# 1 KB weight rows with four open tiles, the gate sums on their own, half of the LayerNorm on ScalarE, and QK half by half

## The chip, the cores and the metric

The kernel runs on one core of one Trainium2 chip. The metric is the device time of one execution in microseconds (us). The kernel before takes 165.44 us, the median of 12 runs that lie between 165.05 and 165.8.

A core has five engines that each follow their own instruction list in order: TensorE (PE, with its weight loads shown apart as PEld), VectorE (DVE), ScalarE (ACT), GpSimd (POOL) and SyncE (SP). They wait for each other by semaphores. SP, ACT and POOL also issue DMAs.

## The reference

The input `x` has 2048 tokens of 512 features in bf16. Two branches are mixed by a gate per token:

```python
g = _sigmoid((x * gate_w).sum(-1, keepdims=True))
a = _A_ref(x, A_wqkv, A_wo)     # local attention
b = _B_ref(x, B_w1, B_b1, B_w2, B_b2)   # MLP over the tokens
return g * a + (1 - g) * b
```

Branch A projects `x` to Q, K and V (32 heads of 16 features). Each token attends to 8 positions: itself and the tokens 2, 4, ... 14 before it. The 8 logits go through a softmax, and the weighted sum of V is multiplied with `wo`. Branch B takes the LayerNorm of `x` over its features, and then mixes tokens: `u = gelu(h^T w1 + b1)` with `w1` of 2048 x 1792, and `y = u w2 + b2` with `w2` of 1792 x 2048.

## The kernel before, in words

The whole problem lies in SBUF at once. The program adds every operation with its engine, its reads and writes and a guessed duration to a scheduler (`_Sched`), which orders the operations on each engine by its guesses, with priorities (`prio`). What comes out is one fixed list per engine, and waits where an operand comes from elsewhere. TensorE's own operations are chained in the order in which they were added (`PE`), apart from the gate and logit sums (`f_sum`), which the scheduler places.

**TensorE** does, in order: a warm-up, transposes of the first tokens, the Q, K and V projections (L649, 176 matmuls of 128x128x512, four to a PSUM bank, each bank followed by a copy out on ACT), the first MLP matmul (L858, operations `ph2_ft_half`: 14 column tiles `ft`, each of two halves of 8 matmuls over the 2048 tokens), the second one (L885, `ph3_i_half`: 16 token tiles, each of two halves of 7 matmuls) and, into the same PSUM bank, the product with `wo` (L894, `wo0` to `wo15`, 4 matmuls each). ACT takes a finished bank out: `gel0` to `gel13` apply the GELU after `ph2`, and `ev0` to `ev15` finish an output tile, which SP stores.

**VectorE** does the attention by itself. Partitions are 32 heads times 4 of a head's 16 features, and `dl` counts the other 4, so that Q K products are elementwise: `qk h_dl_s` multiplies Q with the 8 shifted K for token half h, feature index dl and half s of those 1024 tokens, in 128x4096 elements (512 tokens times 8 shifts). Buffers are P0, P1, P2, each of two halves. The four `dl` are summed by `qa` adds, of which the first two of token half 0 are done by an accumulating DMA on POOL (L747, `qd0_0` and `qd0_1`) instead. `sum0` and `sum1` on TensorE (L722) then add over the 4 partitions of a head, into PSUM banks 4 to 7; 16 matmuls of 32x512 each. The gate's matmuls (L717, 16 of them, bank 3) go in the same operation as `sum0`. ACT copies the logits out (`lev0`), DVE masks them, takes the maximum and subtracts it (`msk`, `mx4`, `mx2`, `mx1`, `msub`), ACT takes the exponential (`exp0`), DVE sums the 8 (`sm4`, `sm2`, `sm1`), ACT takes the logarithm (`lns0`), DVE adds the gate's part (`rsz0`), ACT takes the exponential (`rb0`) and DVE scales (`nrm0`). The same follows for token half 1. `nrm` releases four DMAs on POOL (L790, `av`) that spread the weights, and then DVE multiplies with V (`avm0` to `avm7`, 128x8192) and adds (`ava`, `avb`, `avc`); for u = 3, 4, 5 POOL does the first addition by DMA (L827, `avd`). `wo` of tiles 2u and 2u+1 needs `avc` of u.

DVE also takes the LayerNorm statistics (L692) and applies it to the 16 token tiles (L706, `ln0` to `ln15`).

**ACT's tables**: GELU needs another table set than logarithm and exponential; a load (L954) stands before each change of set. Copy, Relu and Identity need none of their own.

**Weights**: W1 comes in 7 tiles of 256 columns, all 2048 rows (`w1_0` to `w1_6`), and W2 in 8 tiles of 256 columns (`w2_0` to `w2_7`), all on SP's queue in order. `w1_1` and `w1_2` wait for `qd0_1`; `w1_3` and `w1_4` go into the room of the transposed input XT, which the gate's matmuls and the last V projection must have left; `w1_5`, `w1_6` and the W2 tiles go where earlier tiles were. `ebt` is a DMA transpose of the gate's exponentials, also on SP.

PSUM has 8 banks. Q, K and V copies go round over 7 banks, and over banks 0, 1, 2 in the last twelve V projections. `ph2` goes round over 1, 2, 0 (and 3), one open tile after the other:

```python
MLPB = [1, 2, 0, 1, 2, 0, 3, 1, 2, 0, 3, 1, 2, 0]
for ft in range(NFT):
    bank = MLPB[ft]
    for half in range(2):
        PE(f_ph2(ft, bank, half), 1.735, ...)
```

Of the kernel before, what the change touches and what calls it, by code (L numbers as in the profile page):

```python
# [69 lines left out]
class _Sched:  # L70
# [73 lines left out]
    def _pass(self, ops, extra, dma_bw, dma_lat):  # L144
# [21 lines left out]
        dma_free = 0.0  # L166
# [8 lines left out]
        while nleft:  # L175
            best = None
            for e in self.ENGS:
                lst = ready[e]
                if not lst:
                    continue  # L180
                bo = None
                bk = None
                for op in lst:
                    st = max(clock[e], rtime[op.idx])
                    if op.table is not None and loaded is not None and op.table != loaded:
                        st += 1.3
                    k = (st, -bl[op.idx] + 3.0 * op.prio, op.idx)
                    if bk is None or k < bk:
                        bk = k
                        bo = op  # L190
                if best is None or bk < best[0]:
                    best = (bk, bo)
            assert best is not None, "scheduler deadlock (cyclic deps?)"
            st = best[0][0]
            op = best[1]
            e = op.eng
            ready[e].remove(op)
            op.start = st
            if op.table is not None:
                loaded = op.table  # L200
            if op.is_dma:
                clock[e] = st + op.dur
                xs = max(st + 0.3, dma_free)
                xd = max(op.nbytes / dma_bw, 0.05)
                dma_free = xs + xd
                op.end = max(dma_free, clock[e]) + dma_lat
            else:
                op.end = st + op.dur
                clock[e] = op.end
            order[e].append(op)  # L210
            nleft -= 1
            for s_ in op.succ:
                s_.npend -= 1
                if s_.npend == 0:
                    rt = 0.0
                    for d in s_.deps:
                        lat = 0.06 if (d.eng != s_.eng or d.is_dma) else 0.0
                        rt = max(rt, d.end + lat + s_.delay)
                    for d in s_.order:
                        rt = max(rt, d.start + 1e-4)  # L220
                    rtime[s_.idx] = rt
                    ready[s_.eng].append(s_)
# [85 lines left out]
def bass_gated_mix__sliding_local_dilated__mixer_token_mlp__prompt_kernel(nc, A_x, A_wqkv, A_wo, B_x, B_w1, B_b1, B_w2, B_b2, gate_w, out, dbg=None):  # L308
    with contextlib.ExitStack() as es:
# [11 lines left out]
        for b in range(3):  # L321
# [42 lines left out]
        W1H = [view(n_, BF16, [(256, NST), (1, 256)], extra=k_ * W1N)  # L364
               for n_, k_ in (("W1", 0), ("W1", 1), ("W1", 2), ("XT", 0), ("XT", 1), ("W1", 0), ("W1", 1))]
        W1R = ["w1s0", "w1s1", "w1s2", "w1x0", "w1x1", "w1s0", "w1s1"]

        def w2view(name, extra=0):
            return view(name, BF16, [(256, NFT), (1, 256)], extra=extra)
# [166 lines left out]
        def ld_w1(j):  # L536
            w1ld[j] = load("w1_%d" % j, W1H[j], w1v[:, :, 256 * j:256 * j + 256], S * 256 * 2, [W1R[j]] + (XTALL if j in (3, 4) else []), order=j < 3,
                           after=[w1ld[j - 1]] if j > 3 else [])

        def ld_w2(j):  # L540
            w1ld[7 + j] = load("w2_%d" % j, W2S[j], w2v[:, :, 256 * j:256 * j + 256], F * 256 * 2, ["w2_%d" % j] + W2ALIAS[j], order=False,
                               after=[w1ld[6 + j]])
# [162 lines left out]
        for t in range(NST):  # L705
            A("dve", (lambda t_: lambda e: e.tensor_scalar(out=X[:, t_, :], in0=X[:, t_, :], scalar1=col(RSTD, t_), scalar2=col(NMR, t_),  # L706
                                                           op0=ALU.mult, op1=ALU.add))(t), 0.33,
              reads=["rstd", "nmr", "st%d" % t], writes=["x%d" % t], name="ln%d" % t, prio=-10)


        def f_sum(h, b0, with_gate):
            def fn(e):
                ins = None
                if with_gate:
                    for dt in range(4):
                        for c in range(4):
                            ins = e.matmul(ps[32 * c:32 * c + 32, 3, :], lhsT=GWREP[:, dt, :],  # L717
                                           rhs=sub(XT, dt * S + c * UT_, [(HS, 2), (1, UT_)]),
                                           start=(dt == 0), stop=(dt == 3), tile_position=(0, 32 * c))
                for wp in range(4):  # L720
                    for c in range(4):
                        ins = e.matmul(ps[32 * c:32 * c + 32, 4 + wp, :], lhsT=RP, rhs=sub(PB[b0], (c // 2) * 4096 + 2 * wp * 512 + (c % 2) * UT_, [(512, 2), (1, UT_)]),  # L722
# [4 lines left out]
        LGB = ["b4", "b5", "b6", "b7"]  # L727
        PLAN = {0: (0, 1, 2), 1: (1, 2, 0)}
        PS = [["p%d_%d" % (b_, s_) for s_ in range(2)] for b_ in range(3)]
        qkd = {}  # L730
        for h in range(2):
            bb = PLAN[h]

            def qk(dl, b_, s_, h=h):
                sb = 2 * h + s_
                A("dve", tt(sub(PB[b_], s_ * 4096, [(512, NW), (1, 512)]), sub(QH[h], dl * HS + s_ * 512, [(0, NW), (1, 512)]),
                            sub(KH[h], dl * KR + PAD + s_ * 512, [(-2, NW), (1, 512)]), ALU.mult), 2.25,
                  reads=["q%d_%d" % (dl, sb), "k%d_%d" % (dl, sb)] + (["k%d_%d" % (dl, sb - 1)] if s_ else ["khalo" if h else "kpad"]),
                  writes=[PS[b_][s_]], name="qk%d_%d_%d" % (h, dl, s_))

            def qadd(x_, y_, s_, h=h):
                A("dve", tt(sub(PB[x_], s_ * 4096, [(1, 4096)]), sub(PB[x_], s_ * 4096, [(1, 4096)]), sub(PB[y_], s_ * 4096, [(1, 4096)]), ALU.add), 2.25,
                  reads=[PS[y_][s_]], writes=[PS[x_][s_]], name="qa%d_%d%d_%d" % (h, x_, y_, s_))
# [12 lines left out]
            for s_ in range(2):  # L756
                qk(3, bb[1], s_)
                qadd(bb[2], bb[1], s_)
            for s_ in range(2):
                qadd(bb[0], bb[2], s_)  # L760
            b0 = bb[0]
            A("pe", f_sum(h, b0, h == 0), 1.2 + (1.0 if h == 0 else 0), reads=PS[b0] + ["rp"] + ((XTALL + ["gwrep"]) if h == 0 else []),
              writes=LGB + (["b3"] if h == 0 else []), name="sum%d" % h, prio=-100, delay=0.2)
            if h == 0:
                A("act", act(E32, ps[:, 3, :], AF.Relu, scale=-1.0, bias=ZMAX), 0.6, reads=["b3"], writes=["e32"], name="zclip")
                A("act", act(EB, E32, AF.Exp, scale=-1.0, bias=ZMAX), 0.6, reads=["e32"], writes=["eb"], name="zexp", table=LOGEXP)
# [16 lines left out]
            A("dve", tt(ATT[h], ATT[h], sub(RB, 0, [(0, NW), (1, UT_)]), ALU.mult), 1.2, reads=["rb"], writes=["att%d" % h], name="nrm%d" % h, prio=-30)  # L783
# [26 lines left out]
        AVB = (2, 0, 1)  # L810
        avlast = [None]

        def AV(fn, dur, **kw):
            avlast[0] = A("dve", fn, dur, after=[avlast[0]] if avlast[0] else [], **kw)

        def av_parts(u):
            b_ = AVB[u % 3]
# [36 lines left out]
        def f_ph2(ft, bank, half):  # L854
            def fn(e):
                ins = None
                for st in range(8 * half, 8 * half + 8):
                    ins = e.matmul(ps[:, bank, :], lhsT=W1H[ft // 2][:, st, 128 * (ft % 2):128 * (ft % 2) + 128], rhs=X[:, st, :],  # L858
                                   start=(st == 0), stop=(st == NST - 1))
# [3 lines left out]
        MLPB = [1, 2, 0, 1, 2, 0, 3, 1, 2, 0, 3, 1, 2, 0]  # L863
        for ft in range(NFT):
            bank = MLPB[ft]
            for half in range(2):
                PE(f_ph2(ft, bank, half), 1.735, ["x%d" % t for t in range(8 * half, 8 * half + 8)] + [W1R[ft // 2]], ["b%d" % bank],
                   "ph2_%d_%d" % (ft, half))
            A("act", act(UT[:, ft, :], ps[:, bank, :], AF.Gelu_apprx_tanh, bias=col(B1C, ft)), 0.7,
              reads=["b%d" % bank, "b1c"], writes=["ut%d" % ft] + (["wq0", "wq1", "wq2", "wq3", "wk0", "wk1", "wv"] if ft == 0 else []), name="gel%d" % ft, table=GELU)  # L870
            if ft % 2 == 1 and ft // 2 + 5 <= 6:
                ld_w1(ft // 2 + 5)
# [4 lines left out]
        LAG = 5  # L877
        ring[0], ring[1] = 0, [3, 4, 5, 6, 7, 1, 2, 0]
        banks = {}

        def f_ph3(i, bank, half, c0=0, c1=D):
            def fn(e):
                ins = None
                for ft in range(7 * half, 7 * half + 7):
                    ins = e.matmul(ps[:, bank, 0:c1 - c0], lhsT=W2S[i // 2][:, ft, 128 * (i % 2):128 * (i % 2) + 128], rhs=UT[:, ft, c0:c1],  # L885
# [16 lines left out]
        def finish_tile(i):  # L902
            bank = banks[i]
# [5 lines left out]

        L = NST - 1  # L910
        for i in range(L):
            banks[i] = bank_()
        head = ((0, 0), (1, 0), (2, 0), (0, 1), (1, 1), (2, 1))
        for i, half in head + tuple((i, half) for i in range(3, L) for half in range(2)):
            bank = banks[i]
            PE(f_ph3(i, bank, half), 1.52, ["ut%d" % ft for ft in range(7 * half, 7 * half + 7)] + ["w2_%d" % (i // 2)], ["b%d" % bank], "ph3_%d_%d" % (i, half))
            if half == 1 and i >= LAG:
                finish_tile(i - LAG)
        lastb = [bank_(), bank_()]
        CH = ((0, 384), (384, 512))  # L920
        for hf, (c0, c1) in enumerate(CH):
            for half in range(2):
                PE(f_ph3(L, lastb[hf], half, c0, c1), 0.77, ["ut%d" % ft for ft in range(7 * half, 7 * half + 7)] + ["w2_%d" % (L // 2)], ["b%d" % lastb[hf]],
                   "ph3_%d_%d" % (L, half))
        for i in range(L - LAG, L):
            finish_tile(i)
# [92 lines left out]
```

## Time and profile before

| what | value |
|---|---|
| median of 12 runs | 165.44 us (165.05 to 165.8) |
| the profiled execution, its own time | 165.73 us |
| its span | 164.0 us |
| TensorE's granted clock | 1.0 throughout |
| PE busy | 159.4 us, 97% of the span |
| DVE busy | 150.6 us, 92% |
| ACT busy | 70.2 us, 43% |
| DMA moved | 32.24 MB, 197 GB/s on the mean |
| packets under 2 KB | 42,244 of 44,684 |

The profile is of one execution. The span runs from the first to the last instruction that the profile has; the execution's own time has 1.7 us more around it. Busy shares are means over stages with different limits, so that what bounds a stage is read from that stage's waits and not from this table.

### The profile page before, as it was taken

How to read it: one execution, taken by the hardware profiler on the slowest of the kernel's cores; microseconds unless marked ns; L12 is line 12 of the kernel's file. 1: busy time of each engine (PE TensorE's matmuls, PEld its weight loads, DVE VectorE, ACT ScalarE, POOL GpSimd, SP SyncE). 2: the span in 40 equal slices, each digit the busy share in tenths (PEclk: the TensorE clock that was granted, in tenths of full speed). 3: DMA queues.
4: the chain of work that ended last, by engine and by line, in shares of the span. 5: the costliest groups of instructions: out<-in, count | busy, mean ns of one | idle time of the engine just before them, and what ended most of it. 6: DMA issues, size and time to landing. Idle time of an engine off the chain costs nothing.

```text
span 164.0 us, 1989 instructions
## 1 busy us (share of the span) xinstructions
PE 159.4 (97%) x793; PEld 77.5 (47%) x808; DVE 150.6 (92%) x126; ACT 70.2 (43%) x100; POOL 12.0 (7%) x36
## 2 busy tenths in 40 slices
PE   7999999999999999999999999999999999999993
PEld 3755555555544444444444344444444444444641
DVE  0489999899999999999999999999999999999960
ACT  3357677766772379853211257111121111111164
POOL 3000030020000000004000000002200222000000
DMA  5999969809499094999998974990998899991014
GB/s 154 276 242 276 238 155 288 169 0 192 92 301 309 8 249 125 227 290 290 317 240 256 271 203 138 294 240 8 289 229 211 195 208 199 208 215 37 32 58 134
DMA packets 44684, 32.24 MB, mean 197 GB/s; under 512 B 7940, under 2 KB 42244, under 8 KB 44676
## 3 DMA queue, kind: packets, MB, share of 16 engines
q1 hardware_dynamic: 41444, 22.06, 51.9%
q0 software_dynamic: 2512, 9.44, 27.3%
q10 hardware_dynamic: 720, 0.62, 1.1%
q8 instruction: 6, 0.10, 0.2%
q14 instruction: 2, 0.02, 0.0%
HBM read 18.88 MB, written 2.10 MB: 128 GB/s over the span
## 4 chain that ended last, share of the span: by engine, by line
PE 85%; DMA 6%; SPq 6%; ACT 1%; issue 1%
PE ps L858 29%; PE ps L885 29%; PE ps L649 17%; PE ps L894 8%; DMA arena<-in_A_x_dram 6%; SPq L493 4%; SPq L494 1%; PE ps L722 1%; ACT arena L453 1%; PE ps L717 1%; PE ps L604 0%
## 5 line engine op out<-in xcount | busy, mean ns | idle before, releaser
L450 DVE TENSOR_TENSOR arena<-arena 128x4096 bf16<-128x4096 bf16 (+8 forms) x79 | 131.9, 1718 | 1.6 <-ACT arena L453 0.6
L885 PE MATMUL ps<-arena 128*128 128x512 bf16 (+2 forms) x234 | 50.0, 366 | 0.2
L858 PE MATMUL ps<-arena 128*128 128x512 bf16 x218 | 48.5, 379 | 0.3
L453 ACT ACTIVATE arena<-ps,arena 128x512 bf16<-128x512 f32 (+1 forms) x30 | 21.9, 732 | 60.7 <-PE ps L894 37.7
L453 ACT ACTIVATE arena<-ps 128x512 bf16<-128x512 f32 (+3 forms) x53 | 32.9, 629 | 18.4 <-PE ps L649 10.8
L649 PE MATMUL ps<-arena 128*128 128x512 bf16 x173 | 38.0, 379 | 0.2
L885 PEld LDWEIGHTS ps<-arena 128*128 128x128 bf16 x238 | 22.8, 98 | 25.9
L858 PEld LDWEIGHTS ps<-arena 128*128 128x128 bf16 x224 | 21.7, 98 | 26.9 <-issue 0.8
L649 PEld LDWEIGHTS ps<-arena 128*128 128x128 bf16 x176 | 19.9, 113 | 18.0
L894 PE MATMUL ps<-arena 128*128 128x512 bf16 (+2 forms) x67 | 15.6, 366 | 0.1
L453 ACT ACTIVATE arena<-arena 128x16 f32<-128x16 f32 (+5 forms) x10 | 6.7, 678 | 9.7 <-DVE arena L450 9.6
L954 ACT ACT_TABLE_LOAD x7 | 9.0, 1283 | 2.8 <-issue 2.7
L894 PEld LDWEIGHTS ps<-arena 128*128 128x128 bf16 x68 | 6.5, 98 | 7.3
L790 POOL DMA_DIRECT2D arena<-arena x8 | 4.3, 559 | 75.1 <-DVE arena L450 75.1
L692 DVE BATCH_NORM_STATS2 arena<-arena 128x6 f32<-128x512 bf16 x16 | 9.8, 679 | 0.0
L706 DVE TENSOR_SCALAR arena<-arena 128x512 bf16<-128x512 bf16 x16 | 5.3, 406 | 0.0
L579 DVE COPY arena<-ps 128x256 bf16<-128x256 bf16 x4 | 1.1, 292 | 4.5 <-PE ps L567 4.4
L827 POOL DMA_DIRECT2D arena<-arena x3 | 3.6, 1209 | 17.7 <-DVE arena L450 17.7
L747 POOL DMA_DIRECT2D arena<-arena x2 | 2.5, 1268 | 31.6 <-DVE arena L692 21.1
L588 PE MATMUL ps<-arena 128*128 128x256 bf16 (+1 forms) x27 | 4.5, 319 | 0.2
L588 PEld LDWEIGHTS ps<-arena 128*128 128x128 bf16 x28 | 3.1, 121 | 1.1 <-DVE arena L579 0.4
L551 PE MATMUL ps<-const-bfloat16-1.0 128*128 128x512 bf16 (+1 forms) x9 | 2.7, 483 | 0.9 <-PEq L1004 0.9
(30 smaller groups left out, 14.4 us busy)
## 6 DMA issues: line engine op xcount, KB each, us to landing
arena<-in_B_w_dram SPq DMA_DIRECT2D x7, 1024.0 KB, 6.8
arena<-in_B_w_dram SPq DMA_DIRECT2D x8, 896.0 KB, 9.9
arena<-arena POOLq DMA_DIRECT2D x5, 1024.0 KB, 9.6
arena<-arena POOLq DMA_DIRECT2D x8, 512.0 KB, 11.7
out_dram<-arena SPq DMA_DIRECT2D x15, 128.0 KB, 3.1
arena<-in_A_x_dram SPq DMA_DIRECT2D x3, 512.0 KB, 4.7
arena<-in_A_wqkv_dram SPq DMA_DIRECT2D x2, 256.0 KB, 4.4
arena<-in_A_wqkv_dram SPq DMA_DIRECT2D x1, 512.0 KB, 6.5
```

The costliest lines, as they stand in the source:

```text
L450: return lambda e: e.tensor_tensor(out=o_, in0=a_, in1=b_, op=op_)
L453: return lambda e: e.activation(out=o_, in_=i_, func=f_, **kw)
L493: return e.dma_start_transpose(dst, src)
L588: ins = e.matmul(ps[:, dl, c0:c1], lhsT=sub(WQKV, dt * 3 * D + dl, [(4, 128)]), rhs=XT[:, dt, c0:c1], start=(dt == 0 and hb == 0), stop=(d ...
L649: ins = e.matmul(ps[:, bank, :], lhsT=sub(WQKV, dt * 3 * D + tn * D + dl, [(4, 128)]), rhs=XT[:, dt, sb * 512:(sb + 1) * 512], start=(dt = ...
L692: A("dve", (lambda t_: lambda e: e.bn_stats(out=ST6[:, t_, :], in_=X[:, t_, :]))(t), 0.67, reads=["x%d" % t], writes=["st%d" % t], name="s ...
L706: A("dve", (lambda t_: lambda e: e.tensor_scalar(out=X[:, t_, :], in0=X[:, t_, :], scalar1=col(RSTD, t_), scalar2=col(NMR, t_), op0=ALU.mu ...
L790: prev = sch.dma("pool", (lambda d_, s_: lambda e: e.dma_start(d_, s_))(dst, src), 524288, sch.dsem("av%d_%d" % (h, c)), issue=1.0, reads= ...
L858: ins = e.matmul(ps[:, bank, :], lhsT=W1H[ft // 2][:, st, 128 * (ft % 2):128 * (ft % 2) + 128], rhs=X[:, st, :], start=(st == 0), stop=(st ...
L885: ins = e.matmul(ps[:, bank, 0:c1 - c0], lhsT=W2S[i // 2][:, ft, 128 * (i % 2):128 * (i % 2) + 128], rhs=UT[:, ft, c0:c1], start=(ft == 0) ...
L894: ins = e.matmul(ps[:, bank, 0:c1 - c0], lhsT=OT[:, i // 2, dl, 128 * (i % 2):128 * (i % 2) + 128], rhs=WO[:, dl, c0:c1], start=False, sto ...
L954: e.preload_act_table_set(want)
```

## The change

- W1 from the second tile on, and W2, are loaded as tiles of 512 columns and half of the contraction (8 of 16 row blocks for W1, 7 of 14 for W2). A tile keeps its bytes and its place; a row of it is 1 KB where it was 512 B.
- The matmuls follow that: after `ph2_0` and `ph2_1`, groups of four column tiles are run with half 0 for all four and then half 1 for all four, so that four PSUM banks are open. `ph3` goes the same way in groups of four token tiles; the last four are written out by hand (`TAILORDER`).
- The gate's matmuls become an operation of their own (`gate`), added before QK, with `zclip` and `zexp` after it. `sum0` is left with its 16 matmuls. The logit buffers are laid out so that a sum reads 512 contiguous elements.
- `ln8` to `ln15` go to ACT with a scale and a bias from SBUF; `ln0` to `ln7` stay on DVE with a higher priority.
- `qk` and `qa` are added half by half and have priorities. `avm3` stands after `nrm1`; AV buffers are given out in another order.
- The scheduler's model is changed: separate free times for POOL's and the other DMAs, and another rule for which ready operation comes first on ACT.

In the order that comes out, TensorE has the gate between the projections `pjk2_2` and `pjk2_3`, and `sum0` after `ph2_0_0`, `ph2_0_1`, `ph2_1_0` (before: after `ph2_0` and `ph2_1` whole); `sum1` comes before `ph2_13_0`. SP has `ebt` ahead of `w1_1` (before: after `w1_4`). DVE has, after `ln_nmr`: `ln0` to `ln7`, `qk0_0_1`, three small copies (L682 to L684), `qk0_3_0` (which waits for `qd0_0`), `qk0_1_1` (which releases `qd0_1`), `qa0_21_0`, `qa0_02_0`, `qk0_2_1`, `qk1_0_0`, `qk0_3_1` (which waits for `qd0_1`), `qa0_21_1`, `qa0_02_1` (which releases `sum0`), `qk1_1_0`, `qa1_12_0`, `msk` to `msub0`, `qk1_2_0`, `qk1_3_0`, `sm4_0` to `sm1_0`. ACT has `gel0`, `lev0`, `gel1`, `exp0`, `lns0`, `gel2`, `gel3`, `rb0`, `gel4`, `gel5` there, with a table load at each change of set. POOL keeps its list.

```diff
-            return view(name, BF16, [(256, NFT), (1, 256)], extra=extra)
+            return view(name, BF16, [(512, NFT // 2), (1, 512)], extra=extra)
...
-            w1ld[j] = load("w1_%d" % j, W1H[j], w1v[:, :, 256 * j:256 * j + 256], S * 256 * 2, [W1R[j]] + (XTALL if j in (3, 4) else []), order=j < 3,
+            src = w1v[:, 8 * ((j - 1) % 2):8 * ((j - 1) % 2) + 8, 256 + 512 * ((j - 1) // 2):768 + 512 * ((j - 1) // 2)] if j else w1v[:, :, 0:256]
+            w1ld[j] = load("w1_%d" % j, W1H[j], src, S * 256 * 2, [W1R[j]] + (XTALL if j in (3, 4) else []), order=j < 3,
...
         for t in range(NST):
+            if t >= NST - 8:
+                A("act", act(X[:, t, :], X[:, t, :], AF.Identity, scale=col(RSTD, t), bias=col(NMR, t)), 0.6,
+                  reads=["rstd", "nmr", "st%d" % t], writes=["x%d" % t], name="ln%d" % t, prio=8)
+                continue
...
+        A("pe", f_gate, 1.0, reads=XTALL + ["gwrep"], writes=["b3"], name="gate", prio=-100)
+        A("act", act(E32, ps[:, 3, :], AF.Relu, scale=-1.0, bias=ZMAX), 0.6, reads=["b3"], writes=["e32"], name="zclip")
+        A("act", act(EB, E32, AF.Exp, scale=-1.0, bias=ZMAX), 0.6, reads=["e32"], writes=["eb"], name="zexp", table=LOGEXP)
...
             for s_ in range(2):
                 qk(2, bb[2], s_)
-            for s_ in range(2):
                 qk(3, bb[1], s_)
                 qadd(bb[2], bb[1], s_)
-            for s_ in range(2):
                 qadd(bb[0], bb[2], s_)
...
-            A("pe", f_sum(h, b0, h == 0), 1.2 + (1.0 if h == 0 else 0), reads=PS[b0] + ["rp"] + ((XTALL + ["gwrep"]) if h == 0 else []),
-              writes=LGB + (["b3"] if h == 0 else []), name="sum%d" % h, prio=-100, delay=0.2)
+            A("pe", f_sum(b0), 1.0, reads=PS[b0] + ["rp"], writes=LGB, name="sum%d" % h, prio=-100, delay=0.2)
...
-        MLPB = [1, 2, 0, 1, 2, 0, 3, 1, 2, 0, 3, 1, 2, 0]
+        def mlp1(ft, half):
+            bank = (0, 1, 2, 3, 0, 1, 2, 3, 0, 1, 2, 3, 0, 1)[ft]
...
+        for ft in range(2):
+            for half in range(2):
+                mlp1(ft, half)
+        ld_w1(5)
+        for g_ in range(3):
+            for half in range(2):
+                for ft in range(2 + 4 * g_, 6 + 4 * g_):
+                    mlp1(ft, half)
...
+        for b_ in range(3):
             for half in range(2):
+                for i in range(4 * b_, 4 * b_ + 4):
+                    mlp2(i, half)
+                    if half and b_:
+                        finish_tile(i - 4)
```

## The prediction

> **What bounds the kernel now.** I read the page's busy times first, then the chain that ended last in order of time, then each engine's timeline.
>
> ```profile
> PE 159.4 (97%) x793; PEld 77.5 (47%) x808; DVE 150.6 (92%) x126; ACT 70.2 (43%) x100; POOL 12.0 (7%) x36
> PE 85%; DMA 6%; SPq 6%; ACT 1%; issue 1%
> ...
> 47.80 4.32 PE ps L858 x20
> 52.12 0.05 issue
> 52.17 2.54 PE ps L858 x11
> 54.71 0.98 PE ps L717 x16
> 55.68 0.86 PE ps L722 x16
> 56.55 1.40 PE ps L858 x6
> ...
> 92.91 0.98 PE ps L722 x16
> ```
>
> The chain (start, length, what) is TensorE from 19.7 us to 160.5 with no gap but 0.05 us after every 50 or so matmuls. 32 matmuls take 54.71 - 47.80 = 6.91 us, 0.216 each; the 84 from 99.18 to 117.31 (one record is missing) take 0.216 too. So TensorE runs at its own pace in every stage, and DVE at 92% is not waited for: its attention ends at 158.4 (the row that starts at 152.28 lasts 6.13), 1.2 us before `wo14` needs it (156.19 plus 16 of L894's matmuls is 159.65). **The change can win only what it takes out of TensorE's list, and it takes out nothing. It can lose wherever an operand comes late.**
>
> **The Trainium skill.** "TensorE: Matmul & The Clock Gate", section "Back-to-back issue gap", gives N/2.4 + 2.5 ns for an isolated warm matmul, 216 ns for N = 512. The trace agrees (0.216); the 131 ns that the section names for a stream is nowhere in it. "ScalarE: Activation LUTs", section "What ACT_TABLE_LOAD costs", has 1283 ns for a table load and 1380 for a drain. The first is in this trace; the second isn't, as the rows below show. "DMA: Bandwidth & Descriptors", section "Issuing engines are not separate DMA queues", says that all DMAs share the same 16 engines; here the accumulating DMA of POOL took 9.6 us beside W1's first tile and 8.0 alone.
>
> ```profile
> L954 ACT ACT_TABLE_LOAD x7 | 9.0, 1283 | 2.8 <-issue 2.7
> ...
> 71.48 0.42 ACT L453 ACTIVATE arena<-arena 128x256 bf16<-128x256 f32 x1 [2.02 <-DVE arena L450]
> 71.92 1.28 ACT L954 ACT_TABLE_LOAD   x1
> 73.21 1.43 ACT L453 ACTIVATE arena<-ps,arena 128x512 bf16<-128x512 f32 x2
> ...
> 23.34 1.32 POOL L747 DMA_DIRECT2D arena<-arena  x1 [21.12 <-DVE arena L692]
> 35.14 1.21 POOL L747 DMA_DIRECT2D arena<-arena  x1 [10.47 <-DVE arena L450]
> ...
> DMA to landing us min/median/max: 8.0/8.8/9.6
> ```
>
> ACT's timeline: `rb0` ends at 71.90 and the GELU starts at 73.21, so a change of set costs 1.31. POOL's: `qd0_1` lands at 35.14 + 8.0 = 43.15, where SP's waiting W1 load starts; so the 9.6 belongs to `qd0_0`, which lands at 32.98.
>
> **The change, part by part.**
>
> *Gate alone.* Gate and `sum0` together take 0.98 + 0.86; `sum1`, standing alone, takes 0.98. Parted, each costs 0.98: **+0.12 us** on the path. No row shows a lower price; ends 0 and 0.2. The gate's new place makes it wait for the copy L684, done at 31.6; TensorE is there at 33.2 (30.59 and 12 matmuls), so that wait is hidden.
>
> *TensorE's clock.* The gate moves all before `ph2` by 0.98: `ph2_0_0` at 48.78. `sum0` comes after 24 matmuls, 48.78 + 5.18 = 53.96, and ends at 54.94.
>
> *DVE up to `sum0`.* Eight L706 steps are gone: 11 take 3.64 us with 0.40 for the last, 0.324 each, so 2.59 is saved. From 26.46, `ln0` to `ln7` end the stage at 29.05. A 4096-element op steps by 2.20 (starts 32.55, 34.75, 36.96), by 2.31 where the next one needs it. `qk0_0_1` 29.05 to 31.25; the copies L682 to L684 0.37, 31.62. Now `qk0_3_0` needs `qd0_0`, landed at 32.98: **1.4 us of the saving is waited away**. It starts at 33.01, `qk0_1_1` at 35.21, ending 37.49. `qd0_1` is issued 0.31 later as before (34.83 to 35.14), 37.80, and lands at 45.8. Meanwhile `qa0_21_0` 37.41, `qa0_02_0` 39.72, `qk0_2_1` 41.93, `qk1_0_0` 44.13; `qk0_3_1` at 46.33 finds `qd0_1` landed by 0.5. `qa0_21_1` 48.64, `qa0_02_1` 50.96, ending 53.25: 0.7 ahead of TensorE. No wait, but thin.
>
> *The softmax and the GELUs, where the forecast is made.* In the changed list ACT must pass `lns0` and `rb0`, with three changes of set, before `gel4`; and four open banks make `ph2_8_0` take the bank of `ft` 4, so it needs `gel4`. DVE: `qk1_1_0` 53.17, `qa1_12_0` 55.48, `msk` 57.69, then 0.20, 0.69, 0.42, 0.29, 1.23 (rows of 112, 1024, 512, 256, 2048 elements, 0.03 between): 60.66. `exp0` 1.90: 62.59. DVE fills with `qk1_2_0` and `qk1_3_0` and gets to the three sums at 64.98; 1.22 + 0.69 + 0.42 + 0.06: 67.38. ACT: `lns0` 67.41 to 67.83, change of set, `gel2` 69.14 to 69.83, `gel3` (0.10 of it over the one before) to 70.43, change, `rb0` 71.74 to 72.16, change, `gel4` 73.47 to **74.16**. TensorE reaches `ph2_8_0` after 88 more matmuls, 54.94 + 19.01 = **73.95**. It is 0.21 short, and then its weight load (98 ns), hidden otherwise, lies open, with a hand-over of as much: **+0.43 us**. Ends: 0 if the chain of 17 steps runs 0.4 early; 1.4 if 1 us late, since each delay of DVE is paid one to one. Before, `gel4` was due far later than done (67.74), since three banks went round with one tile open.
>
> *After that.* `sum1` 89.9 against DVE's 89.0; `gel13` 105.0 against `ph3_0_1` at 106.1. Both hold and shift together with TensorE. DVE ends 1.2 us earlier, at 157.2; nothing waits for that.
>
> *LayerNorm on ACT.* Nearest row: L453's Identity with two pointers, 0.78 (the same page's price: 186 + 427 + two times 93 ns, 0.80). Copies of 0.60 step by 0.49 (two take 1.08 from 9.79). Two copies and one LayerNorm are 2 x 0.49 + 0.68 = 1.66, within the 1.73 that two projections take: hidden by ACT's idle time of 0.27 per projection. In the three-bank stretch only `ln15` and `zexp` remain; a bank is wanted 1.73 after it fills. `ln8` waits for L703, done at 26.42, and ACT gets to it at 27.6, so the copies behind it aren't held up. I take 0; at most 0.3.
>
> *Edits at no cost.* `zclip` and `zexp` leave the softmax stage for the same idle time of ACT. QK half by half moves which adds come when, not how many: counted above. `avm3` after `nrm1`, and the AV buffers, move DVE work that has 1.2 us and more to spare. `ph3` in groups of four, and the hand-written tail, keep all matmuls and their widths; the banks they take again were emptied by `ev` one group, some 10 us, earlier.
>
> *1 KB rows.* The same 14 MB; fewer packets. TensorE waited for no weight before, so 0 gain. SP: `ebt` now holds the queue 3.72 us from 43.0, when `zexp` is done, to 46.8, ahead of `w1_1`, which before took 43.15 to about 50.2. Landing 7.05 later, 53.9, against `ph2_2_0` at 56.67: hidden with 2.8 to spare. Behind it `w1_2`, `wo`, `w1_3` to `w1_6` follow with more room; `w1_3` no longer waits for the gate at `sum0`. W2's tiles start on `ph2`'s groups and have 7 us or more. POOL's `av` follow `nrm0` at 75.5, the first lands 8 us on, before `avm0` at 89.5. Stores and `ev` keep their spacing; the tail after the last matmul (3.5 us) is the same.
>
> **Sum:** 0.12 + 0.43 = +0.55. The profiled execution took 165.73 (164.0 and 1.7 around), 0.29 above the median, and none of its parts waits, so I add to the median: 165.44 + 0.55 = **166.0 us**.
>
> **Rivals.** A difference under 0.2%, 0.33 us, can't be told from none.
> - *A, the forecast:* `gel4` late; 165.7 to 166.8. Chance 0.58.
> - *B, all covers hold:* +0.12, 165.56. It decides if DVE's chain from `qd0_0` on is 0.4 us faster than I add up, for which a landing of `qd0_0` in 9.2 speaks. Against: DVE has no other gap to give. 0.25, within 0.2%.
> - *C, faster:* the 0.05 us gaps in TensorE's stream, some 15 of them, 0.75 in all, come of memory traffic and go with half the packets: 0.12 - 0.75, 164.8. Against: the piece from 30.59 to 41.32 has the same 50 matmuls between two gaps although DMAs stood still from 32.5 to 36.7. 0.07.
> - *D, `qd0_1` late:* `ebt` shares the DMA engines with its end. From a landing beyond 47.0 (9.2 us) `sum0` waits too. The longest of POOL's accumulating DMAs (L827) took 12.8: landing 50.6, `sum0` 3.6 late, and `gel4`'s wait on top: 169.6. Against: 8.0 when alone. 0.10.
>
> **Numbers.** Likeliest 166.0. The range holds A and B, and D's milder half: 165.4 to 167.2. Faster 0.07 (C), same 0.25 (B), slower 0.68 (A and D).
>
> **What would show it.** Right: TensorE idle once before L858 at about 74 us, released by ACT; DVE idle 1.4 us near 31.6, released by a DMA; the 0.98 twice. Wrong: no PE gap, or one before `sum0` (D), or matmuls stepping by less than 0.216 (C).

## The result, and the profile after

The changed kernel takes **167.09 us** (median of 11 runs, 166.36 to 167.77), and the kernel before, beside it on the same chip, 165.51 (47 runs). The ratio is 1.0094, with a 95% interval of 1.0080 to 1.0108: **1.58 us slower**, where 0.55 was forecast. It lies inside the range, and the sign is right; the size is not.

The page of the changed kernel first: busy times, then the shares of the chain that ended last, then the rows that changed.

```profile
PE 159.4 (97%) x793; PEld 77.0 (47%) x808; DVE 148.6 (90%) x118; ACT 79.4 (48%) x112; POOL 12.0 (7%) x36
...
q1 hardware_dynamic: 28132, 22.06, 45.7%
...
PE 56%; DVE 20%; DMA 14%; ACT 5%; issue 3%
...
L452 DVE TENSOR_TENSOR arena<-arena 128x4096 bf16<-128x4096 bf16 (+7 forms) x79 | 132.5, 1719 | 4.1 <-DMA arena<-arena 2.3
...
L974 ACT ACT_TABLE_LOAD x11 | 14.1, 1283 | 2.9 <-issue 2.7
```

Of the kernel before, DVE's row and the weights' queue:

```profile
q1 hardware_dynamic: 41444, 22.06, 51.9%
...
L450 DVE TENSOR_TENSOR arena<-arena 128x4096 bf16<-128x4096 bf16 (+8 forms) x79 | 131.9, 1718 | 1.6 <-ACT arena L453 0.6
```

PE is as busy as before. What is new is in the chain: it was TensorE for 85% of its length, and is now TensorE for 56%, with DVE, a DMA and ACT in between. DVE's own row says why: it stood idle 2.3 us for a DMA, which it did not do before. The chain in order of time (start, length, what) names the places:

```profile
22.57 9.82 DMA arena<-arena
32.39 0.02 issue
32.42 4.51 DVE arena L452 x2
36.92 0.30 issue
37.22 9.69 DMA arena<-arena
46.91 0.02 issue
...
67.59 0.43 DVE arena L452
68.05 0.42 ACT arena L455
68.47 0.02 issue
68.48 1.28 ACT L974
69.77 0.01 issue
69.78 1.26 ACT arena L455 x2
71.04 0.02 issue
71.06 1.28 ACT L974
72.34 0.01 issue
72.36 0.42 ACT arena L455
72.77 0.02 issue
72.79 1.28 ACT L974
74.07 0.01 issue
74.08 0.69 ACT arena L455
74.78 0.05 issue
74.83 5.79 PE ps L867 x26
```

Read it downwards: `qd0_0` (9.82 us), `qk0_3_0` and `qk0_1_1`, `qd0_1` (9.69 us), DVE's products and the softmax, then ACT with `lns0`, a change of table, `gel2` and `gel3`, a change, `rb0`, a change, `gel4`. Only then TensorE's `ph2_8_0`, at 74.83. DVE's timeline and TensorE's, in two stretches each, give the sizes of the waits in brackets:

```profile
32.42 13.43 DVE L452 TENSOR_TENSOR arena<-arena 128x4096 bf16<-128x4096 bf16 x6 [1.23 <-DMA arena<-arena]
46.94 9.14 DVE L452 TENSOR_TENSOR arena<-arena 128x4096 bf16<-128x4096 bf16 x4 [1.09 <-DMA arena<-arena]
```

```profile
53.94 1.05 PE L731 MATMUL ps<-arena 128*32 128x512 bf16 x16 [0.30 <-DVE arena L452]
...
74.83 3.41 PE L867 MATMUL ps<-arena 128*128 128x512 bf16 x15 [0.68 <-ACT arena L455]
```

Matmul ends are modelled, so the size of a TensorE wait is better read from the step between the starts of two matmuls, 0.216 us in a packed stream. In the changed kernel the steps that are longer than in the kernel before add up to 1.49 us: the gate's way in and out 0.19, the next step behind the gate 0.03, `sum0` 0.375, `ph2_6_0` 0.054, `ph2_8_0` 0.840. (The 0.03 belongs to the gate: every kernel here with the gate alone has that step at 0.24 us, and the two with the gate beside `sum0` have not.) Steps of 0.432, twice 0.216, are matmuls whose record is missing; the "0.05 issue" pieces of the chain lie at those places. TensorE's last matmul is 1.08 us later than before, since its projections happened to start 0.45 us earlier in this execution.

### The profile page after: what moved, and what is told of

Same layout as the page of the kernel before. It is cut to its first block, busy times and chain, and to the rows that moved or that the text cites. A ratio compares the mean times of both kernels' runs of the same rounds, so it can differ in the third digit from the quotient of the medians.

```text
span 165.1 us, 1990 instructions
## 1 busy us (share of the span) xinstructions
PE 159.4 (97%) x793; PEld 77.0 (47%) x808; DVE 148.6 (90%) x118; ACT 79.4 (48%) x112; POOL 12.0 (7%) x36
## 3 DMA queue, kind: packets, MB, share of 16 engines
q1 hardware_dynamic: 28132, 22.06, 45.7%
## 4 chain that ended last, share of the span: by engine, by line
PE 56%; DVE 20%; DMA 14%; ACT 5%; issue 3%
PE ps L899 29%; DVE arena L452 16%; PE ps L867 15%; DMA arena<-arena 12%; PE ps L908 8%; DVE arena L695 4%; ACT arena L455 3%; ACT L974 2%; PE ps L591 2%; DMA arena<-in_A_x_dram 2%; PE ps L570 1%; PE ps L652 1%; PE ps L731 1%; DVE arena L582 0%
## 5 line engine op out<-in xcount | busy, mean ns | idle before, releaser
L452 DVE TENSOR_TENSOR arena<-arena 128x4096 bf16<-128x4096 bf16 (+7 forms) x79 | 132.5, 1719 | 4.1 <-DMA arena<-arena 2.3
L455 ACT ACTIVATE arena<-arena 128x512 bf16<-128x512 bf16 (+6 forms) x18 | 13.2, 734 | 9.1 <-DVE arena L452 9.0
L591 PE MATMUL ps<-arena 128*128 128x256 bf16 (+1 forms) x27 | 3.8, 287 | 0.2
```

What stands on the lines that cost most here:

```text
L452: return lambda e: e.tensor_tensor(out=o_, in0=a_, in1=b_, op=op_)
L455: return lambda e: e.activation(out=o_, in_=i_, func=f_, **kw)
L591: ins = e.matmul(ps[:, dl, c0:c1], lhsT=sub(WQKV, dt * 3 * D + dl, [(4, 128)]), rhs=XT[:, dt, c0:c1], start=(dt == 0 and hb == 0), stop=(d ...
```

## The experiments

Each kernel has its orders fixed by a list of names, so that only what its diff shows differs. Lines in these kernels stand 9 further on than in the changed kernel (DVE's adds and products are L461, the sums L740, `ph2` L876).

A ratio is always to the kernel before on the same chip, timed beside it. Four chips were used: one for e1 to e4, one for e5, e6, e9 and e10, one for e7, e11 and e12, one for e13. e4_both and e12_both_again are the same program, and their ratios on two chips lie 0.0031 apart, 0.51 us. So a difference of half a microsecond between kernels of different chips may be the chips'.

### `rb0` behind `gel5`, or two more banks

```diff
 ScalarE: lns0 gel2 gel3
-rb0 gel4 gel5
+gel4 gel5 rb0
```

> The changed kernel with all orders kept, but rb0 stands behind gel4 and gel5 on ACT, so that two of the three changes of table set before gel4 fall away; ebt is where the change put it. Theory T: gel4 is done at about 71.7 us, the wait of 0.84 before ph2_8_0 is gone, the one before sum0 (0.38) stays, and sum1 may now wait 0.1 for DVE; 0.75 us below the changed kernel, about 166.35. Rival V: another wait ends at the same place and the time stays at 167.1.

Measured: 166.51 us, ratio 1.0068 (1.0046 to 1.0090).

```diff
-bank = (0, 1, 2, 3, 0, 1, 2, 3, 0, 1, 2, 3, 0, 1)[ft]
+bank = (0, 1, 2, 3, 0, 1, 2, 3, 4, 5, 2, 3, 0, 1)[ft]
```

> The changed kernel with all orders kept, ACT's with its changes of table set too, but ph2_8 and ph2_9 are summed in PSUM banks 4 and 5 (free between lev0 and sum1) instead of 0 and 1, so that ph2_8_0 no longer needs gel4. Theory T (the bank is what ties TensorE to gel4): gel4 is as late as in the changed kernel, TensorE does not wait for it, and the time is 0.75 us below, about 166.35, as with rb0 moved. Rival W (the table loads themselves cost, wherever TensorE looks): 167.1.

Measured: 166.56 us, ratio 1.0065 (1.0047 to 1.0083). Two different ways to free `ph2_8_0` from `gel4` give the same: 1.0094 less 1.0068 or 1.0065 is 0.43 or 0.48 us, each give or take 0.4 by the two intervals, where 0.75 was expected. In both profiles TensorE passes 74 us without a wait. **The wait for `gel4` is confirmed; its size in time is known only roughly.** Some 1.1 us remain.

### `ebt` behind `w1_4`, and both

```diff
 SyncE: w1_0
-ebt w1_1 w1_2 wo w1_3 w1_4
+w1_1 w1_2 wo w1_3 w1_4 ebt
```

> The changed kernel with all orders kept, but ebt (the DMA transpose of the gate's exponentials) stands behind w1_4 on SP, where it was before the change. Theory T (the transpose holds up the last packets of qd0_1, and DVE's delay is paid one to one): qd0_1 lands about 8.0 us after its issue instead of 9.7, DVE no longer waits before qk0_3_1 (1.1 us less), TensorE's wait before sum0 (0.38) is gone and that before ph2_8_0 falls from 0.84 to 0.1 or so; time 1.1 us below the changed kernel, about 166.0. Rival U (qd0_1 is slow for another reason, in place of the transpose): still 9.7 us, and 167.1. Rival V (the two waits don't set the end): qd0_1 is faster but the time stays at 167.1.

Measured: 166.95 us, ratio 1.0079 (1.0053 to 1.0104), hardly better than the changed kernel. Its profiled execution took 165.76, the shortest of its six; there `qd0_1` took 8.4 us instead of 9.7.

> The changed kernel with ebt behind w1_4 and rb0 behind gel5. Theory T: no wait of TensorE from sum0 on; what is left against the kernel before is the gate standing alone (0.19, by the steps between matmuls at its two ends) and a wait of 0.03 in the projections: 0.2 to 0.3 above before, 165.7. If some cost of the change lies elsewhere (LayerNorm on ACT, weight rows), it shows here as more than 0.3.

Measured: 166.27 us, ratio 1.0045 (1.0029 to 1.0060), 0.74 us above the kernel before where 0.2 to 0.3 was expected; profiled 165.05, the shortest of 22, with `qd0_1` at 8.2 us and no wait from `sum0` on. Since the profile fell on the shortest execution, the same kernel ran once more:

> The same kernel as e4_both, run beside the other two, for a second look and a second profile: the profiled execution of e4_both, 165.05 us, was the shortest of its 22, so its profile may not show what the median execution waits for. If qd0_1 takes 9 us or more in this profile and TensorE waits at sum0, the landing differs from execution to execution although ebt is out of the way; if it takes 8.2 to 8.4 us again and nothing waits, the loss is somewhere that the profile does not show. Time 166.0 to 166.5 us.

Measured: 166.55 us, ratio 1.0076 (1.0053 to 1.0099), profiled 166.34. `qd0_1` took 8.95 us, a little under the 9 that the first branch names, and TensorE waited at `sum0`. The chain of this execution, and DVE's timeline:

```profile
16.46 4.75 DMA arena<-in_A_x_dram
21.21 0.02 issue
21.24 1.89 DVE arena L704 x3
23.13 0.46 issue
23.59 9.66 DMA arena<-arena
33.25 0.02 issue
33.27 4.50 DVE arena L461 x2
37.78 0.30 issue
38.08 8.95 DMA arena<-arena
47.02 0.02 issue
...
54.00 0.04 issue
54.04 1.05 PE ps L740 x16
```

```profile
33.27 13.43 DVE L461 TENSOR_TENSOR arena<-arena 128x4096 bf16<-128x4096 bf16 x6 [1.25 <-DMA arena<-arena]
47.05 9.14 DVE L461 TENSOR_TENSOR arena<-arena 128x4096 bf16<-128x4096 bf16 x4 [0.35 <-DMA arena<-arena]
```

DVE's timeline of e4_both, the same program:

```profile
31.37 24.81 DVE L461 TENSOR_TENSOR arena<-arena 128x4096 bf16<-128x4096 bf16 x11 [0.62 <-DMA arena<-arena]
```

`ebt` is out of the way in both, and yet `qd0_1` took 8.21 us in one and 8.95 in the other. So `ebt` can't be the sole cause. But most of the difference is older than `qd0_1`. In the second execution a load of `x` came late to DVE's statistics (L704, at 21.24), `qd0_0` was issued at 23.59 instead of 21.92, and `qk0_3_0` began at 33.27 instead of 31.37. That is 1.90 us of the 2.34 by which `qk0_3_1` was later; the wait for `qd0_1` is only 0.35 of them. Since `qk0_3_0` waits for `qd0_0`, what delays `qd0_0` delays all of DVE's chain.

**For the slower `qd0_1`, the trace's list of packets shows a second candidate beside `ebt`.** Once in this stretch a 16 KB packet of queue q8, which the page calls "instruction", occupies a DMA engine for 0.9 to 1.0 us; I call it the fetch. The DMA table of the execution above, for 37 to 48 us, has it beside the 272 packets of `qd0_1` (q0):

```profile
q0 software_dynamic: 272, 1.05, 53.1%
q8 instruction: 1, 0.02, 0.6%
```

All the profiles, sorted by the time of `qd0_1` (us; from the packets' starts and the DMA's issue and landing):

| kernel | issue | last packet | fetch | landing | took |
|---|---|---|---|---|---|
| e13_swap | 34.53 | 42.02 | 41.94 to 42.95 | 42.37 | 7.84 |
| before | 35.14 | 42.81 | 43.87 to 44.75 | 43.13 | 7.99 |
| e4_both | 36.17 | 43.98 | 43.98 to 44.96 | 44.38 | 8.21 |
| e9_slack | 37.25 | 44.99 | 44.99 to 45.89 | 45.55 | 8.30 |
| e6_gate_sum0 | 37.54 | 45.43 | 45.43 to 46.38 | 45.90 | 8.36 |
| e10_slack_gate | 37.47 | 45.38 | 45.38 to 46.34 | 45.87 | 8.40 |
| e1_ebt_late | 36.88 | 44.80 | 44.80 to 45.76 | 45.29 | 8.41 |
| e5_ln_dve | 38.93 | 47.18 | 41.70 to 42.72 | 47.53 | 8.60 |
| e12_both_again | 38.08 | 46.67 | 42.48 to 43.46 | 47.02 | 8.94 |
| e7_sum0_late | 37.62 | 46.55 | 44.83 to 45.79 | 46.99 | 9.37 |
| after | 37.22 | 46.18 | 44.87 to 45.83 | 46.91 | 9.69 |
| e2_rb0_late | 37.06 | 44.94 | 44.94 to 45.84 | 46.75 | 9.69 |
| e3_banks45 | 37.24 | 45.20 | 45.20 to 46.16 | 47.02 | 9.78 |
| e11_sums_early | 37.84 | 46.46 | 45.58 to 46.47 | 47.65 | 9.81 |

First the ten profiles in which `ebt` was not beside `qd0_1`, all but the changed kernel, e2_rb0_late, e3_banks45 and e5_ln_dve. Where the fetch begins with the last packet of `qd0_1` (within 0.1 us) or after it, `qd0_1` took 7.8 to 8.4 us, in seven of them. In three the fetch got in ahead of the last packets, and it took 8.9 to 9.8. In e12_both_again the table of 45.56 to 46.8 us shows the laggards: three 4 KB packets and the closing one.

```profile
DMA packets 4, 0.01 MB, mean 10 GB/s; under 512 B 1, under 2 KB 1, under 8 KB 4
```

The trace also keeps 16 reports of completion for `qd0_1`, which I take as one from each DMA engine. In these three profiles 15 come together and one alone, 1.1 to 2.0 us behind (e12_both_again: 45.67 to 45.89, and 47.02). That is what one held engine would give.

With `ebt` beside `qd0_1` the reports look different. In the changed kernel the closing packets of 15 engines had started by 44.98, yet all 16 reports come between 46.79 and 46.91, just as the last of `ebt`'s 512 packets of 256 B end (46.87). The fetch held one closing packet up to 46.18, but was not what came last. In e2_rb0_late and e3_banks45 the fetch was not ahead at all, and still 6 and 11 of the 16 reports come only at 46.7 to 47.0, when `ebt`'s packets end (46.72 and 46.97). (In e5_ln_dve, too, all 16 come together, at 47.41 to 47.53.) And on the one chip of e1 to e4, `qd0_1` took 9.69 and 9.78 in the two kernels with `ebt` early, 8.41 and 8.21 in the two with `ebt` late. So by these times it was **`ebt` that set the landing** in the changed kernel's own profile, and the fetch is the candidate for the kernels in which `ebt` is late.

The limits of this reading: no kernel moves the fetch alone. The three profiles with the fetch ahead and no `ebt` are all of one chip, and none of the undisturbed ones is known to be of that chip. In eight profiles the fetch begins within 0.1 us of the last packet, so that its time may itself depend on `qd0_1`. And which of the two was at work in the executions that were only timed, no record shows.

### The cover: the places of the sums

What one microsecond of `qd0_1` costs depends on how long TensorE has other work.

The first kernel gives it back the work that it had, against the changed kernel (and `ebt` stands behind `w1_4`; from `avm0` on VectorE has the order of the kernel before):

```diff
 TensorE: ph2_0_1
-ph2_1_0 sum0 ph2_1_1
+ph2_1_0 ph2_1_1 sum0
...
-ph2_12_0 sum1 ph2_13_0 ph2_10_1
+ph2_12_0 ph2_13_0 ph2_10_1 sum1
 ScalarE: gel0 lev0 gel1 exp0
-lns0 gel2 gel3 rb0 gel4 gel5
+gel2 gel3 gel4 gel5 lns0 rb0
...
-lev1 gel10 exp1 gel11 gel12 lns1 gel13 rb1
+gel10 lev1 gel11 gel12 gel13 exp1 lns1 rb1
 VectorE: qa1_02_0
-rsz0 qa1_10_0 qk1_0_1 nrm0 qk1_1_1 qa1_12_1
+qa1_10_0 qk1_0_1 qk1_1_1 rsz0 qa1_12_1 nrm0
```

> This kernel keeps the 1 KB rows, the four open tiles, the gate alone amid Q and K, the eight LayerNorm tiles on ScalarE and QK half by half. It puts back what gives TensorE other work while VectorE finishes: sum0 stands after ph2_1_1 and sum1 after ph2_10_1, as in the kernel before; ebt is issued behind w1_4; on ScalarE lns0 and rb0 come behind gel5 and the levs, exps and gels alternate as before; VectorE's order from avm0 on is that of the kernel before. Theory of lost slack (the changed kernel has lowered the time that VectorE and ScalarE may be late at sum0, gel2, sum1 and gel13 from about 2 us to 0 to 0.9 us, and each execution in which a transfer lands later pays for it): only the gate's two extra block changes are left, 0.19 us by the steps between matmuls, so 165.7 us where the kernel before has 165.5, ratio 1.0005 to 1.002, and a smaller scatter than the changed kernel's. Rival (the rows of 1 KB or the work on ScalarE cost time by themselves, whatever the order): what e4_both kept of the loss stays, 166.2 us or more, ratio 1.004 or more.

Measured: 165.84 us, ratio 1.0026 (1.0014 to 1.0038), the runs within 0.41 us of each other: the rival's 1.004 lies outside the interval, and the theory's 1.002 in it.

Against this kernel, the sums alone go back to the places of the changed one:

```diff
 TensorE:
-ph2_1_0 ph2_1_1 sum0
+ph2_1_0 sum0 ph2_1_1
...
-ph2_12_0 ph2_13_0 ph2_10_1 sum1
+ph2_12_0 sum1 ph2_13_0 ph2_10_1
```

> e9_slack with one thing put back as the changed kernel has it: TensorE takes sum0 after ph2_1_0 (8 matmuls, 1.7 us, earlier) and sum1 after ph2_12_0 (16 matmuls, 3.5 us, earlier). TensorE does the same work, and VectorE and ScalarE keep their orders. Theory of lost slack: at sum0 the attention has only 0.4 to 0.7 us to spare now and at sum1 less than 1, so executions in which a transfer lands late pay: 0.2 to 0.5 us over e9_slack, with a wider scatter. Rival (the places of the sums cost nothing, and what e9_slack gained on e4_both came from the order on ScalarE and VectorE): within 0.1 us of e9_slack.

Measured: 166.40 us, ratio 1.0060 (1.0043 to 1.0076), 13 runs between 165.53 and 167.06. 1.0060 less 1.0026 is 0.56 us, and the spread is wider (1.53 us over 13 runs, 0.41 over 8), as the theory had it. In its profile `qd0_1` took 9.81, and TensorE stands at `sum0`:

```profile
54.67 1.05 PE L740 MATMUL ps<-arena 128*32 128x512 bf16 x16 [0.68 <-DVE arena L461]
```

**That the early places alone cost 0.56 us is not shown, though.** The two kernels ran on different chips, and 0.51 us is what the same program differed by. On one chip, e6_gate_sum0 below, with both sums early, stands level with e10_slack_gate, whose sums are late (1.0012 and 1.0009). What the profiles show is the wait: TensorE stood at `sum0` in four of the ten with `sum0` early, for 0.375 us in the changed kernel, 0.55 in e5_ln_dve, 0.68 in e12_both_again and 0.75 in e11_sums_early, by the steps.

And against e4_both, `sum0` alone goes to its place of before:

```diff
 TensorE:
-ph2_1_0 sum0 ph2_1_1
+ph2_1_0 ph2_1_1 sum0
```

> e4_both with sum0 alone moved back to the place of the kernel before, after ph2_1_1; sum1 and all other orders stay. The attention gains 1.7 us at sum0, but lev0, exp0 and all that follows on ScalarE move later by 0.65 us. Theory of lost slack, with sum0 as the thin point: 0.2 to 0.4 us under e4_both. Rival (the thin points are behind it, at gel2, sum1 and gel13, and a later sum0 makes them thinner): the same as e4_both or up to 0.3 us more.

Measured: 166.63 us, ratio 1.0083 (1.0059 to 1.0107), beside the 1.0076 of the same kernel without the move on the same chip. The rival is right as far as this can be told: moving `sum0` alone shows no gain. The step before `ph2_6_0` (`gel2`) is 0.634 in its profile (0.276 in e12_both_again), and `sum1` and `ph3_0_1` are late too; the wait goes to the next thin place.

### The gate, and the LayerNorm

The gate goes back beside `sum0`, once against e9_slack and once against e4_both (`zclip` then stands ahead of `lev0` and `zexp` ahead of `exp0` on ScalarE):

```diff
 TensorE: pjk2_2
-gate pjk2_3
+pjk2_3
...
-sum0
+gate sum0
```

The gate is 16 matmuls; the 64 that two expectations name is wrong.

> e9_slack, and the gate's 64 matmuls put back beside sum0, so that the change into blocks of 32 columns and out of them is paid once less. Theory: 0.19 us under e9_slack, 165.5 us, level with the kernel before (ratio 0.999 to 1.001). Rival (the block changes are hidden or cost nothing in time): the same as e9_slack within 0.1 us. If rows and ScalarE work cost time by themselves, this kernel too stays 0.4 us or more above the kernel before.

Measured: 165.58 us, ratio 1.0009 (1.0000 to 1.0018). From 1.0026: 0.28 us for the gate's standing alone. The steps say where: from 128-column matmuls into the 32-column ones 0.309, out again 0.312, each some 0.09 over 0.216, and 0.24 for the step after that.

> e4_both, and the gate's 64 matmuls directly ahead of sum0, in one stretch with it, at sum0's early place. TensorE saves one change into and out of blocks of 32 columns (0.19 us), and sum0 starts later in TensorE's order by the gate's own length. Theory: 0.19 us under e4_both, 166.1 us, and a little more if the gate's time ahead of sum0 covers a late VectorE. Rival (the gate's results, zclip and zexp, now come late on ScalarE and hold lev0 or the norm): 166.3 us or more.

Measured: 165.56 us, ratio 1.0012 (0.9998 to 1.0025). That is 0.55 us under e4_both, where 0.19 was expected. The two ran on different chips, and why the gain is larger stays open.

The LayerNorm tiles go back to VectorE, against the changed kernel:

```diff
 VectorE: gwrep b1c b2c
+ln8 ln9 ln10 ln11 ln12 ln13 ln14 ln15
 qk0_3_0 qk0_1_1
```

> The changed kernel with one part undone: the LayerNorm tiles ln8 to ln15 are on VectorE again, right behind the statistics, ahead of qk0_3_0. They take 2.6 us there, of which about 1.2 us fill the idle time in which qk0_3_0 waits for qd0_0, so VectorE comes about 1.4 us later to everything up to sum0. Theory of lost slack: there is none left at sum0, so nearly all of it is paid: 0.9 to 1.4 us more than the changed kernel, 168.0 to 168.5 us. Rival (VectorE still has the 2 us of slack of the kernel before, and the loss comes from ScalarE's work or the rows): no later than the changed kernel, 167.1 us or less.

Measured: 167.47 us, ratio 1.0128 (1.0115 to 1.0141). That is 0.56 us over the changed kernel by the ratios and 0.38 by the medians, where the theory had 0.9 to 1.4. DVE's timeline shows my mistake:

```profile
31.55 2.67 DVE L722 TENSOR_SCALAR arena<-arena 128x512 bf16<-128x512 bf16 x8
34.13 22.57 DVE L461 TENSOR_TENSOR arena<-arena 128x4096 bf16<-128x4096 bf16 x10
```

The tiles fill both idle stretches, 1.23 and 1.09 us; I had counted the first. 2.6 less 2.3 leaves 0.3. So putting half of the LayerNorm on ACT gave DVE 2.6 us, and the changed order lost 2.3 of them to waiting.

### Two neighbours swapped

DVE waits at 31.2 us for `qd0_0` with `qk0_1_1` ready behind, and `qd0_1` can't be issued before `qk0_1_1` is done. In the kernel before, `qk0_1_1` came first and `qk0_3_0` fourth. Against the changed kernel:

```diff
 VectorE: gwrep b1c b2c
-qk0_3_0 qk0_1_1 qa0_21_0
+qk0_1_1 qk0_3_0 qa0_21_0
```

> The changed kernel with two neighbours on VectorE swapped: qk0_1_1 is taken ahead of qk0_3_0, and nothing else is moved (ebt, rb0, the gate, both sums and the LayerNorm tiles stay as the change has them). In the changed kernel VectorE stands idle for 1.23 us until qd0_0 lands, with qk0_1_1 ready behind it, and qd0_1 cannot be issued before qk0_1_1 is done. Theory (the late issue of qd0_1 brings its last packets to where a 16 KB instruction fetch stands in the same DMA engine, and the attention has no room for it): qd0_1 is issued some 3 us earlier, at about 34.1 us, and lands before 44 us, ahead of the fetch; VectorE loses both of its waits, 2.3 us; sum0 and gel4 are then in time, by about 1.5 and 0.4 us. What is left is the gate's price, 0.2 to 0.3 us, and at most 0.2 more: 165.5 to 165.8 us against 165.35 before, ratio 1.001 to 1.003. Rival (what costs lies behind sum0, in the changes of table on ScalarE with rb0 ahead of gel4, and in sum1's early place, whatever VectorE's head start): at least what e2_rb0_late or e4_both kept, 166.1 us or more, ratio 1.0045 or more.

Measured: **165.72 us, ratio 1.0008 (0.9992 to 1.0024)**. POOL's, DVE's and TensorE's timelines, and the DMA table of 34 to 46 us:

```profile
34.53 1.21 POOL L770 DMA_DIRECT2D arena<-arena  x1 [10.39 <-DVE arena L461]
```

```profile
31.93 24.93 DVE L461 TENSOR_TENSOR arena<-arena 128x4096 bf16<-128x4096 bf16 x11
```

```profile
54.40 1.05 PE L740 MATMUL ps<-arena 128*32 128x512 bf16 x16
55.38 24.99 PE L876 MATMUL ps<-arena 128*128 128x512 bf16 x115
```

```profile
arena<-arena POOLq DMA_DIRECT2D x1, 1024.0 KB, 7.8
```

`qd0_1` is issued 2.7 us earlier and takes 7.8; eleven products and adds follow each other with no wait; and no TensorE step is long any more except at the ways into and out of the sums and the gate, although `rb0` still stands ahead of `gel4`, `ebt` ahead of `w1_1`, and both sums early. **One swap takes back 1.0094 less 1.0008, 1.42 us of the 1.58**, give or take 0.35, which is more than chips were seen to differ by. It takes both of DVE's waits away at once (`qk0_3_0` finds `qd0_0` landed, and `qd0_1` lands at 42.37, before `ebt`'s packets begin at 44.74), so it does not tell their shares apart. The profiled execution, 166.38, was the longest of its 14: the projections came 0.84 us later in it than in the changed kernel's (gate at 33.44 and 32.60), and nothing after them waited. The fetch did not stay where it was: it began at 41.94, with the last packet. No version beats the kernel before: TensorE's list has the same matmuls, and the gate apart costs on top.

## Why the prediction was right or wrong

**Right.** TensorE's own pace bounds the kernel, so the change could only lose. *1.4 us of the saving is waited away*: 1.23. *`gel4`*: the chain of 17 steps was late, and taking the wait away gave 0.43 and 0.48 us for the 0.43 forecast. That the sizes agree is luck in part: the forecast was 0.21 of lateness and 0.22 of weight load and hand-over, and in the profile `gel4` ended 0.79 after TensorE was ready (74.77 and 73.98), with 0.05 from there to the matmul. *LayerNorm on ACT*: 0.80 each for 0.78, and no step of TensorE at the projections is longer for it. *1 KB rows*: q1 has a third fewer packets (41,444 before), and 45.7% of the engines' time instead of 51.9%, and nobody waited for a weight. The kernel with rows, open tiles, LayerNorm and QK as changed, but with cover and the gate beside `sum0`, stands at 1.0009.

**The step that failed: "lands at 45.8".** I carried over the 8.0 us of the kernel before for `qd0_1`, because the DMA had been alone then. It was issued at 37.22, 0.58 earlier than my 37.80, and landed at 46.91, 1.1 later: it took 9.69. My own times had `ebt` on SP's queue from 43.0 to 46.8, beside the end of `qd0_1`, and I still gave `qd0_1` the time of a DMA that is alone. Rival D had the mechanism, `ebt`, with `sum0` to wait from a landing beyond 47.0; the landing was 46.91 and the wait began there, in an execution whose projections came early (in e3_banks45 it was 47.02, the projections came 0.7 us later, and `sum0` did not wait). I gave D 0.10. The cost then came twice, as D said: 0.375 at `sum0`, and `gel4`'s wait grew in the profile to 0.84, because DVE's chain reached `sm1_0` at 68.02 instead of 67.38.

**The thin cover was seen and not priced.** The text has "no wait, but thin" at `sum0`, and 0.2 at `gel4`. In two executions of one program `qd0_0` landed at 31.34 and 33.25, and `qd0_1` took 8.21 and 8.94. Against such differences a cover of 0.7 fails in some executions even if the one profile that I had shows no wait. What that is worth in the median is not measured by itself: of the 1.58 us, `gel4` and the gate account for some 0.45 and 0.28, and how the rest divides stays open. That nearly all of it hangs on DVE's waits for the two DMAs is what e13_swap shows.

**The gate** was 0.12 forecast, 0.22 by the steps, 0.28 in time (give or take 0.25). The lengths in the chain of waits that I subtracted end where the next piece starts, and part of the way out lies in the next piece.

**Rival C** is refuted: the 0.05 gaps are places of missing records, and the four profiles that have all 808 matmuls (e7, e11, e12, e13) have no step of 0.432. **Rival B** would have held if `qd0_1` had been early; e13_swap is nearly that kernel, and its 1.0008 agrees with B's +0.12.

*`ebt` holds SP for 3.72 us*: it was 1.55, and `w1_1` landed at 52.4 for 53.9; hidden either way. DVE ended at 157.9 for 157.2.

## What to carry to other kernels

When a faster part of a chain stops at a DMA, look at what stands behind the waiting instruction: here the ready product behind it was what the next DMA waited for, and one swap took back nine tenths of the loss. When a DMA moves in time, don't take its old duration along; list what else is on the DMA engines at the new time. And a cover that is smaller than the scatter of the transfers above it is not free, even where the sum says "in time": give it a price, as an estimate.

## What the runs showed of the hardware

- A 16 KB packet of the instruction queue (q8) takes 0.88 to 1.02 us at 42 to 46 us of the 14 profiles. The Trainium skill, "DMA: Bandwidth & Descriptors", section "Issuing engines are not separate DMA queues", has all DMAs share 16 engines; the trace agrees: three profiles with this packet ahead of the end of a 1 MB accumulating DMA have one of its 16 reports late, and it took 8.9 to 9.8 us instead of 7.8 to 8.4. That the packet is the cause is argued from this.
- A DMA transpose of 512 packets of 256 B at the end of that DMA goes with a time of 9.7 to 9.8 us (three profiles): most or all of the late reports come when the transpose's packets end, up to 1.8 us after the DMA's own last packet.
- Going from 128-column matmuls to 32-column ones and back costs TensorE some 0.09 us at each step (0.309 and 0.312 us instead of 0.216).
- A matmul without a record looks like 0.05 us of "issue" in the chain of waits; the step of 0.432 gives it away.
